# One linear-attention and two-MoE kernel: keys prepared for two pairs of heads together, and split tiles of double size in a ring of two

## The chip, the core and the metric

The kernel runs on one core of one Trainium2 chip. The metric is the device time of one execution in microseconds; three runs of the kernel before took 1551.31, 1551.88 and 1555.19 us, so the median is 1551.88 us. Five engines take part: TensorE (PE; its weight loads are recorded apart, as PEld), VectorE (DVE), ScalarE (ACT), GpSimd (POOL, which here mainly issues DMAs) and SyncE (SP, which issues most DMAs). Each engine runs its own queue in program order, and waits for the others by semaphores.

## The reference, cut to what matters

```python
q_s = exp(q - max(q, axis=-1)); q_s = q_s / (sum(q_s, axis=-1) + 1e-9)   # q, k, v: 8 x 8 x 576 x 64, fp32
k_s = exp(k - max(k, axis=2));  k_s = k_s / (sum(k_s, axis=2) + 1e-9)     # over the 576 positions
kv = einsum('bhsd,bhse->bhde', k_s, v)
x = einsum('bhsd,bhde->bhse', q_s, kv)        # transposed to 4608 tokens x 512
x = relu(x @ w_in)**2 @ w_out                 # 512 -> 2048 -> 512, first layer
x = elu(x @ w_in2) @ w_out2                   # the same sizes, second layer
```

## The kernel before, in words

**Products.** Every fp32 operand of the two layers is split into a high and a low half (fp32r), and a product is three matmuls: high x high, high x low, low x high. The 4608 tokens are nine blocks of 512, t = 0 to 8. In block 0 the first layer is computed directly. From block 1 on, the first product of the layer (`up`, L652 to L654) runs in 16 chunks of 12 matmuls for each block; its result is in one of two banks of PSUM, tag "ph", and ScalarE takes it out with a relu (L661), so TensorE cannot begin chunk c + 2 before the relu of chunk c is done. The second product is a Strassen-Winograd scheme of 7 products on pairs of blocks (1, 2), (3, 4), (5, 6), (7, 8): 56 units u of 6 matmuls (`u_mm`, L773). A unit needs a tile w1 (`u_load`, L751, from the DRAM tensors w1s) and a split of the activations (`u_split`: uh on ScalarE, L760, ul on VectorE, L761). The second layer uses seven products for both matrices (L934, L1049) from 840 us on, and the change doesn't reach into it.

**Attention.** Batch b is 576 positions, its 8 heads are 4 pairs of 128 columns. For each pair: `kt_load` (L244, the transposed keys, one buffer), `k_max` (VectorE, L282, the maximum over the positions, one number per column), `k_load` and `v_load` (L256, L274, two buffers each), `k_row` (one transpose on TensorE, L288, which lays the maxima along a row), `k_sub` (VectorE, L295), `k_exp` (ScalarE, L300), `kv_mm` (L309: ten matmuls of 65 columns that use half of the array's columns each; the extra column of ones in vr gives the sums), `kv_sum`, `kv_inv` (VectorE, three tiny operations) and `kv_out` (ScalarE, two tiny copies with a scale). The rows of maxima, the k-v products, the transposes of q and the x products share two banks of PSUM (tag "att").

**Weight sums.** The Winograd scheme needs seven sums of quarters of the weights, split too. `s_hi` writes a high half with ScalarE (L199, L202), `s_lo` the low half with VectorE (L210, L215), and each half goes to DRAM (w1s, w2s, w3s) by a DMA that GpSimd issues (L203, L216; L211 for the quarter that stands alone, k = 3, where one tile holds both halves). The tiles come from one ring, tag "st", with five buffers of 128 x 512 fp32. The ring also serves the four tiles o of block 0's result (`y_out`, L692 to L695) and the loads of units 2 and 3 (`u_load`; in pair (1, 2) these two take a buffer of another tag, "raw"). A tile of the ring is given out again when the DMA that reads it has landed, or the matmul that reads it is done.

**Order.** Everything is issued in the order in which the code is written; there is no scheduler behind it. `attention(t)` fills 32 slots with the steps of the next key batch and query block. `place_all` and `place_turns` spread the slots over chunks and units of earlier blocks, and the sums of weights, the outputs and the rest of the Winograd additions (`u_out`, `u_rest`) are put at chunks by hand. At each chunk or unit the program emits its matmuls first and then what was put there, so a step that waits on ScalarE holds up the relus behind it, and one on VectorE the splits behind it.

Of the kernel before, what the change touches and what calls it, by code (L numbers as in the profile page):

```python
# [20 lines left out]
def tile_attention_moe_moe2(  # L21
# [172 lines left out]
        return quarters(w, j)[i], s_home(w, j)[:, to]  # L194

    def s_hi(w, j, k):
        hi = pool.tile([P, DM], F32R, tag="st", bufs=5, name=f"sh{w}_{j}_{k}").rearrange("p (i n) -> p i n", n=HW)
        if k == 3:
            nc.scalar.activation(hi[:, 0], s_alone(w, j)[0], AF.Copy)  # L199
        else:  # L200
            x, d = s_source(w, j, k)
            nc.scalar.activation(hi, x, AF.Copy)  # L202
            nc.gpsimd.dma_start(d[:, :, 0, :], f32(hi))  # L203
        parts[w, j, k] = hi

    def s_lo(w, j, k):
        hi = parts.pop((w, j, k))
        if k == 3:
            x, d = s_alone(w, j)
            nc.vector.tensor_tensor(hi[:, 1], x, f32(hi[:, 0]), op=ALU.subtract)  # L210
            nc.gpsimd.dma_start(d, f32(hi))  # L211
        else:
            x, d = s_source(w, j, k)
            lo = pool.tile([P, DM], F32R, tag="st", bufs=5, name=f"sl{w}_{j}_{k}").rearrange("p (i n) -> p i n", n=HW)
            nc.vector.tensor_tensor(lo, x, f32(hi), op=ALU.subtract)  # L215
            nc.gpsimd.dma_start(d[:, :, 1, :], f32(lo))  # L216

    def s_copy(w, j):

# [58 lines left out]
    chunks = ((0, S // P, P), (S // P, SC, S % P))  # L278

    def k_max(b, p):  # L280
        m = att.tile([P, 1], F32, tag="km", bufs=2, name=f"km{b}_{p}")
        nc.vector.tensor_reduce(m, st.pop(("kt", b, p)), axis=AX.X, op=ALU.max)  # L282
        st["km", b, p] = m

# [17 lines left out]
    def kv_mm(b, p):  # L302
        ks, vr = st.pop(("k", b, p)), st.pop(("v", b, p))


        pk = bank([P, D + 1], f"pk{b}_{p}")
        for c in range(SC):
            for j in range(2):
                nc.tensor.matmul(  # L309
                    pk[j * D : (j + 1) * D],  # L310
                    ks[:, c, j * D : (j + 1) * D],
                    vr[:, c, j * (D + 1) : (j + 1) * (D + 1)],
                    start=(c == 0),
                    stop=(c == SC - 1),
                    tile_position=(0, j * D),
                )
        kv = att.tile([P, D], F32, tag="kvs", bufs=2 * NP, name=f"kvs{b}_{p}")
        kvs[b, p] = kv
        st["pk", b, p] = pk

    def kv_sum(b, p):
        z = att.tile([P, 1], F32, tag="kz", bufs=2, name=f"kz{b}_{p}")
# [136 lines left out]
    def attention(t):  # L459

        slots, put = plan()
        new = [b for b, _, _ in pieces(t) if b not in begun]
        begun.update(new)

        far = t > 1
        for b in new:
            for p in range(NP):
                for i, f in (
                    (0, kt_load), (2, k_max), (5, k_load), (5, v_load), (8, k_row), (8, k_sub), (9 + far, k_exp),
                    (11 + far, kv_mm), (11 + far, kv_sum), (11 + far, kv_inv), (11 + 2 * far, kv_out),  # L470
                ):
                    if p == NP - 1 and (f is kv_out if far else i == 11):
                        i = 12
                    if f is kt_load and p and not far:
                        i = (-3, -3, -2)[p - 1]
                    put(i + 4 * p, f, b, p)
        for s in range(NS):
            put(s // 2 if far else (0, 2, 6, 11)[s], q_load, t, s)
            for i, f in (
                (2, q_max), (3, q_sub), (4 + far, q_exp), (5 + 2 * far, q_sum), (6 + 2 * far, q_eps),  # L480
                (7 + 2 * far, q_inv), (7 + 2 * far, q_norm),
            ):
                put(i + 5 * s, f, t, s)
        turns = ((25, 28), (26, None), (29, 31), (30, None)) if far else ((25, 27), (26, None), (28, 29), (28, None))
        for p, (i, j) in enumerate(turns):
            if j is not None:
                put(j, x_mm, t, p)
            put(i, x_tr, t, p)
        return slots
# [8 lines left out]
    )  # L498

    def k0_max(p):  # L500
        m = att.tile([P, 1], F32, tag="km", bufs=2, name=f"km0_{p}")
        nc.vector.tensor_reduce(m, st["kt", 0, p], axis=AX.X, op=ALU.max, negate=True)
        st["km", 0, p] = m

# [171 lines left out]
    def down(layer, t, j):  # L676
# [3 lines left out]
        for c in range(NP):  # L680
# [4 lines left out]
            nc.tensor.matmul(y[c], hi[:, cs], gl, start=False, stop=False)  # L685
            nc.tensor.matmul(y[c], lo[:, cs], gh, start=False, stop=last)
            if last and t < NB - 1:
                y_out(t, c, pool.tile([P, TB], F32, tag="st", bufs=5, name=f"o{layer}_{t}_{c}"))

    def y_out(t, c, o):  # L690
        if c % 2 == 0 or (t, c) == (0, 1):
# [50 lines left out]
    def u_load(t, u):  # L742
        if u < NU:
            i, j = SEVEN[u // NG][0], u % NG
            tag, bufs = ("at", 2) if u < 2 else ("st", 5) if u < 4 else (("xh", "xl")[u % 2] + str(u % 8 // 2), 1)
            if t == PAIRED and 1 < u < 4:
                w = keep.tile([P, 2 * DM], F32R, tag="raw", bufs=3, name=f"w1_{t}_{u}")
                w = w[:, 0:DM].rearrange("p (s k f) -> p s k f", s=2, f=P)
            else:
                w = pool.tile([P, 2, 2, P], F32R, tag=tag, bufs=bufs, name=f"w1_{t}_{u}")  # L750
            nc.sync.dma_start(f32(w), w1s[j][:, i].rearrange("p s (k f) -> p s k f", f=P))  # L751
# [419 lines left out]
    with tc.manual_schedule():  # L1171
# [29 lines left out]
        for t in range(PAIRED, NB - 2, 2):  # L1201
# [14 lines left out]
                place(firsts[t + 2][0], u_out, t, 4, 0, 1, t, m)  # L1216
                place(firsts[t + 2][1], u_out, t, 0, 1, 0, t, m)
            place(firsts[t + 2][2], u_rest, t, 6, 0, t + 1)
            place(firsts[t + 2][4], u_rest, t, "v", 1, t + 1)


        late = [(0, "c", s) for s in (NSL - 2, NSL - 1)] + firsts[1] + firsts[2][:-2]
# [158 lines left out]
```

## Time and profile before

| what | value |
|---|---|
| runs | 1551.31, 1551.88, 1555.19 us, median 1551.88 |
| the profiled execution | 1550.84 us, of which the span of the trace is 1549.1 |
| TensorE busy | 1529.8 us, 99% of the span, granted clock 1.000 |
| VectorE, ScalarE, GpSimd busy | 1226.8 us (79%), 1016.0 us (66%), 129.4 us (8%) |
| chain that ended last | TensorE 87%, VectorE 6%, ScalarE 3%, DMA 2%, issue 1% |
| k-v products, all blocks (L309) | 560 matmuls recorded, 22.5 us busy |
| rows of maxima (L288) | 28 transposes, 8.5 us busy |

How to read it: matmuls are pipelined, so the duration of one in the trace (0.39 us for 512 columns) is longer than the distance between two starts, and the ends are modelled. The cost of something that stands between matmuls is therefore read from starts. A row of the timeline gives the start and the duration in us, the engine, line and operation, "out<-in" by the program's names, the shape, how many instructions are drawn together (x20), and in brackets how long the engine was idle before it and what released it. Two forms of matmul are recorded as two each, so the ten of `kv_mm` stand as x20.

### The profile page before, as it was taken

How to read it: one execution, taken by the hardware profiler on the slowest of the kernel's cores; microseconds unless marked ns; L12 is line 12 of the kernel's file. 1: busy time of each engine (PE TensorE's matmuls, PEld its weight loads, DVE VectorE, ACT ScalarE, POOL GpSimd, SP SyncE). 2: the span in 40 equal slices, each digit the busy share in tenths (PEclk: the TensorE clock that was granted, in tenths of full speed). 3: DMA queues.
4: the chain of work that ended last, by engine and by line, in shares of the span. 5: the costliest groups of instructions: out<-in, count | busy, mean ns of one | idle time of the engine just before them, and what ended most of it. 6: DMA issues, size and time to landing. Idle time of an engine off the chain costs nothing.

```text
span 1549.1 us, 25531 instructions
## 1 busy us (share of the span) xinstructions
PE 1529.8 (99%) x9056; PEld 1320.3 (85%) x9056; DVE 1226.8 (79%) x1803; ACT 1016.0 (66%) x1621; POOL 129.4 (8%) x202
## 2 busy tenths in 40 slices
PE   7999999999999999999999999999999999999999
PEld 5778787877778787887888889988998899999998
DVE  8998597787778787886687897679777976887785
ACT  7976665577565765656564885388538853874873
POOL 1002220032011310032201000000000000000000
PEclk9999999999999999999999999999999999999999
DMA  9857566677576775845686676867676768888876
GB/s 266 252 162 260 204 221 203 236 251 245 168 251 232 260 251 164 263 175 184 219 274 211 196 245 184 242 193 246 185 241 194 234 184 245 276 269 281 262 246 207
DMA packets 200768, 351.68 MB, mean 227 GB/s; under 512 B 20161, under 2 KB 67265, under 8 KB 200641
## 3 DMA queue, kind: packets, MB, share of 16 engines
q1 hardware_dynamic: 186096, 302.71, 64.2%
q0 software_dynamic: 14400, 47.20, 7.7%
q8 instruction: 73, 1.20, 0.3%
q14 instruction: 55, 0.44, 0.1%
q10 hardware_dynamic: 144, 0.13, 0.0%
HBM read 287.05 MB, written 62.91 MB: 226 GB/s over the span
## 4 chain that ended last, share of the span: by engine, by line
PE 87%; DVE 6%; ACT 3%; DMA 2%; issue 1%; POOL 0%; SPq 0%; DVEq 0%; POOLq 0%; ACTq 0%
PE y L1049 23%; PE p L934 22%; PE p L773 17%; PE ph L652 7%; PE ph L653 7%; PE ph L654 7%; PE px L429 1%; PE pk L309 1%; PE pt L401 1%; DVE ul L761 1%; DMA kt<-kt_dram 1%; DVE T L737 0%; DVE B L737 0%; DVE mt_wi L126 0%; ACT raw_wi L120 0%
## 5 line engine op out<-in xcount | busy, mean ns | idle before, releaser
L1049 PE MATMUL y<-w,dh 128*128 128x256 f32 x2016 | 358.7, 281 | 0.0
L934 PE MATMUL p<-x2h,w 128*128 128x512 f32 (+1 forms) x1120 | 322.2, 368 | 0.0
L1049 PEld LDWEIGHTS y<-w,dh 128*128 128x128 f32 x2016 | 309.6, 188 | 0.1
L1049 PE MATMUL y<-w,dl 128*128 128x256 f32 x1008 | 283.9, 282 | 0.2
L773 PE MATMUL p<-uh,w 128*128 128x512 f32 x896 | 281.8, 392 | 0.0
L934 PEld LDWEIGHTS p<-x2h,w 128*128 128x128 f32 x1120 | 207.1, 188 | 27.4 <-DVE g L975 1.1
L652 PE MATMUL ph<-xh,wi0h 128*128 128x512 f32 x576 | 229.6, 399 | 0.0
L653 PE MATMUL ph<-xl,wi0h 128*128 128x512 f32 x576 | 225.1, 391 | 0.7 <-DVE xl L590 0.6
L654 PE MATMUL ph<-xh,wi0l 128*128 128x512 f32 x576 | 224.7, 390 | 0.4 <-DVE wi0l L149 0.3
L934 PE MATMUL p<-x2l,w 128*128 128x512 f32 (+1 forms) x560 | 205.6, 367 | 0.0
L773 PEld LDWEIGHTS p<-uh,w 128*128 128x128 f32 x896 | 168.2, 188 | 36.9 <-issue 2.0
L1049 PEld LDWEIGHTS y<-w,dl 128*128 128x128 f32 x1008 | 189.7, 188 | 1.1 <-DVE dl L1026 0.9
L1020 ACT ACTIVATE dh<-g 128x1024 fp32r<-128x1024 f32 (+1 forms) x120 | 116.3, 974 | 112.0 <-PE y L1049 109.9
L760 ACT ACTIVATE uh<-B 128x512 fp32r<-128x512 f32 x192 | 121.0, 632 | 97.5 <-PE p L773 71.9
L773 PE MATMUL p<-ul,w 128*128 128x512 f32 x448 | 176.2, 393 | 0.7 <-DVE ul L761 0.4
L1026 DVE TENSOR_TENSOR dl<-g,dh 128x1024 fp32r<-128x1024 f32 (+1 forms) x120 | 133.7, 1115 | 45.2 <-ACT dh L1020 44.8
L761 DVE TENSOR_TENSOR ul<-B,uh 128x512 fp32r<-128x512 f32 x192 | 130.3, 688 | 46.2 <-ACT uh L760 45.4
L661 ACT ACTIVATE B<-ph 128x512 f32<-128x512 f32 x128 | 76.3, 596 | 119.9 <-PE ph L654 116.2
L652 PEld LDWEIGHTS ph<-xh,wi0h 128*128 128x128 f32 x576 | 109.0, 189 | 28.4 <-issue 3.9
L654 PEld LDWEIGHTS ph<-xh,wi0l 128*128 128x128 f32 x576 | 108.2, 188 | 24.8 <-DVE wi0l L149 1.6
L653 PEld LDWEIGHTS ph<-xl,wi0h 128*128 128x128 f32 x576 | 108.3, 188 | 22.7 <-DVE xl L590 1.8
L996 DVE SCALAR_TENSOR_TENSOR t<-e,t 128x1024 f32<-128x1024 f32 (+3 forms) x85 | 89.9, 1058 | 33.8 <-ACT e L992 33.4
(155 smaller groups left out, 2298.7 us busy)
## 6 DMA issues: line engine op xcount, KB each, us to landing
w<-w2s SPq DMA_DIRECT2D x280, 256.0 KB, 3.3
w<-w3s SPq DMA_DIRECT2D x280, 256.0 KB, 3.0
w<-w1s SPq DMA_DIRECT2D x224, 256.0 KB, 3.8
raw_wo<-wo_dram SPq DMA_DIRECT2D x32, 512.0 KB, 4.3
vr<-v_dram SPq DMA_DIRECT2D x32, 320.0 KB, 5.8
kt<-kt_dram SPq DMA_DIRECT2D x32, 288.0 KB, 4.2
q<-q_dram SPq DMA_DIRECT2D x36, 256.0 KB, 4.6
ks<-k_dram SPq DMA_DIRECT2D x28, 320.0 KB, 4.7
```

Source lines behind the costliest of these rows:

```text
L652: nc.tensor.matmul(ph, hi[:, c], xh[p], start=(p == 0), stop=False)
L653: nc.tensor.matmul(ph, hi[:, c], xl[p], start=False, stop=False)
L654: nc.tensor.matmul(ph, lo[:, c], xh[p], start=False, stop=(p == NP - 1))
L661: nc.scalar.activation(g, ph, AF.Relu)
L760: nc.scalar.activation(hi, x, AF.Copy)
L761: nc.vector.tensor_tensor(lo, x, f32(hi), op=ALU.subtract)
L773: nc.tensor.matmul(accs[side, m], w[:, s, m], x, start=(new and (j, s) == (0, 0) and x is hi), stop=(j == NG - 1 and s == 1), skip_group_c ...
L934: nc.tensor.matmul(acc, w[:, s, c], x[:, k], start=(begin and (k, s) == (0, 0) and x is hi), stop=((k, s) == (1, 1)), skip_group_check=not ...
L996: nc.vector.scalar_tensor_tensor(g, e, 1.0, g, ALU.add, ALU.mult)
L1020: nc.scalar.activation(hi, x, AF.Copy)
L1026: nc.vector.tensor_tensor(lo, x, f32(hi), op=ALU.subtract)
L1049: nc.tensor.matmul(y2[side, b][:, a * HW : (a + 1) * HW], x[:, u % 2, at], w[:, s], start=(new and (j, s, a) == (0, 0, 0) and x is hi), st ...
```

## The change

1. **Ring.** `s_hi` and `s_lo` share one tile of 128 x 1024 for k = 0, 1, 2, high and low half beside each other for each i; one DMA goes out, after the low half, where there were two. The ring "st" has two buffers of that size, and k = 3 has a buffer of its own, "st1". Two tiles o share one tile of the ring, and so do the loads of units 2 and 3.
2. **Keys of two pairs together, from block t = 2 on (`far`).** `k_rows` makes the rows of maxima of two pairs in one bank, and `kv2_mm` the k-v products of two pairs, with `kv2_sum`, one `kv_inv` and `kv2_out`. km has four buffers. The slots: kt_load 0, 3, 7, 10 (before 0, 4, 8, 12), k_max 3, 6, 10, 13 (before 2, 6, 10, 14), the loads of k and v of both pairs at 7 and 15 (before 5, 9, 13, 17), k_rows 10 and 18, k_sub 10, 11, 18, 19, k_exp 12, 13, 20, 21, the product at 15 and 23, its copies at 16 and 24.
3. **Block 1** (not `far`): of the last pair, k_load, v_load, k_row, k_sub, k_exp and kv_out come one slot earlier, kv_mm, kv_sum and kv_inv two.
4. **`u_rest`**: the sum v and its two DMAs stand at chunk 9 of the block after the pair, where they stood at chunk 4.

**The diff** (lines that are only "..." stand for what is left out; kv2_sum adds 1e-9 to the two sums as kv_sum does).

```diff
--- before.py
+++ after.py
...
         return quarters(w, j)[i], s_home(w, j)[:, to]
 
     def s_hi(w, j, k):
-        hi = pool.tile([P, DM], F32R, tag="st", bufs=5, name=f"sh{w}_{j}_{k}").rearrange("p (i n) -> p i n", n=HW)
         if k == 3:
+            hi = pool.tile([P, DM], F32R, tag="st1", name=f"sh{w}_{j}_{k}").rearrange("p (i n) -> p i n", n=HW)
             nc.scalar.activation(hi[:, 0], s_alone(w, j)[0], AF.Copy)
         else:
-            x, d = s_source(w, j, k)
-            nc.scalar.activation(hi, x, AF.Copy)
-            nc.gpsimd.dma_start(d[:, :, 0, :], f32(hi))
+            hi = pool.tile([P, 2 * DM], F32R, tag="st", bufs=2, name=f"sh{w}_{j}_{k}")
+            hi = hi.rearrange("p (i s n) -> p i s n", s=2, n=HW)
+            nc.scalar.activation(hi[:, :, 0], s_source(w, j, k)[0], AF.Copy)
         parts[w, j, k] = hi
 
     def s_lo(w, j, k):
...
             nc.gpsimd.dma_start(d, f32(hi))
         else:
             x, d = s_source(w, j, k)
-            lo = pool.tile([P, DM], F32R, tag="st", bufs=5, name=f"sl{w}_{j}_{k}").rearrange("p (i n) -> p i n", n=HW)
-            nc.vector.tensor_tensor(lo, x, f32(hi), op=ALU.subtract)
-            nc.gpsimd.dma_start(d[:, :, 1, :], f32(lo))
+            nc.vector.tensor_tensor(hi[:, :, 1], x, f32(hi[:, :, 0]), op=ALU.subtract)
+            nc.gpsimd.dma_start(d, f32(hi))
 
     def s_copy(w, j):
 
...
-        m = att.tile([P, 1], F32, tag="km", bufs=2, name=f"km{b}_{p}")
+        m = att.tile([P, 1], F32, tag="km", bufs=NP, name=f"km{b}_{p}")
...
+
+    def k_rows(b, p):
+        pm = bank([P, 2 * P], f"pm{b}_{p}")
+        for i in range(2):
+            row = st["pm", b, p + i] = pm[:, i * P : (i + 1) * P]
+            nc.tensor.transpose(row, st.pop(("km", b, p + i)).to_broadcast([P, P]), ident)
+
+    def kv2_mm(b, p):
+        pk = bank([P, 2 * (D + 1)], f"pk{b}_{p}").rearrange("p (i n) -> p i n", i=2)
+        for i in range(2):
+            ks, vr = st.pop(("k", b, p + i)), st.pop(("v", b, p + i))
+            for c in range(SC):
+                for j in range(2):
+                    nc.tensor.matmul(
+                        pk[j * D : (j + 1) * D, i],
+                        ks[:, c, j * D : (j + 1) * D],
+                        vr[:, c, j * (D + 1) : (j + 1) * (D + 1)],
+                        start=(c == 0),
+                        stop=(c == SC - 1),
+                        tile_position=(0, j * D),
+                    )
+        st["pk", b, p] = pk
+
...
+    def kv2_out(b, p):
+        pk, z = st.pop(("pk", b, p)), st.pop(("kz", b, p))
+        for i in range(2):
+            kv = kvs[b, p + i] = att.tile([P, D], F32, tag="kvs", bufs=2 * NP, name=f"kvs{b}_{p + i}")
+            for j in range(2):
+                r = slice(j * D, (j + 1) * D)
+                nc.scalar.activation(kv[r], pk[r, i, 1 - j : 1 - j + D], AF.Copy, scale=z[r, i : i + 1])
 
     def kv_sum(b, p):
         z = att.tile([P, 1], F32, tag="kz", bufs=2, name=f"kz{b}_{p}")
...
         far = t > 1
         for b in new:
             for p in range(NP):
+                if far:
+                    put((0, 3, 7, 10)[p], kt_load, b, p)
+                    put((3, 6, 10, 13)[p], k_max, b, p)
+                    h = p // 2 * 8
+                    if p % 2 == 0:
+                        put(10 + h, k_rows, b, p)
+                    for f, i in ((k_load, 7), (v_load, 7), (k_sub, 10 + p % 2), (k_exp, 12 + p % 2)):
+                        put(i + h, f, b, p)
+                    if p % 2:
+                        for i, f in ((15, kv2_mm), (15, kv2_sum), (15, kv_inv), (16, kv2_out)):
+                            put(i + h, f, b, p - 1)
+                    continue
                 for i, f in (
-                    (0, kt_load), (2, k_max), (5, k_load), (5, v_load), (8, k_row), (8, k_sub), (9 + far, k_exp),
-                    (11 + far, kv_mm), (11 + far, kv_sum), (11 + far, kv_inv), (11 + 2 * far, kv_out),
+                    (0, kt_load), (2, k_max), (5, k_load), (5, v_load), (8, k_row), (8, k_sub), (9, k_exp),
+                    (11, kv_mm), (11, kv_sum), (11, kv_inv), (11, kv_out),
                 ):
-                    if p == NP - 1 and (f is kv_out if far else i == 11):
-                        i = 12
-                    if f is kt_load and p and not far:
+                    if p == NP - 1:
+                        i -= f in (k_load, v_load, k_row, k_sub, k_exp, kv_mm, kv_sum, kv_inv)
+                    if f is kt_load and p:
                         i = (-3, -3, -2)[p - 1]
                     put(i + 4 * p, f, b, p)
         for s in range(NS):
...
     )
 
...
             if last and t < NB - 1:
-                y_out(t, c, pool.tile([P, TB], F32, tag="st", bufs=5, name=f"o{layer}_{t}_{c}"))
+                if c % 2 == 0:
+                    st["o"] = pool.tile([P, 2, TB], F32, tag="st", bufs=2, name=f"o{layer}_{t}_{c}")
+                y_out(t, c, st["o"][:, c % 2])
 
     def y_out(t, c, o):
         if c % 2 == 0 or (t, c) == (0, 1):
...
     def u_load(t, u):
         if u < NU:
             i, j = SEVEN[u // NG][0], u % NG
-            tag, bufs = ("at", 2) if u < 2 else ("st", 5) if u < 4 else (("xh", "xl")[u % 2] + str(u % 8 // 2), 1)
-            if t == PAIRED and 1 < u < 4:
-                w = keep.tile([P, 2 * DM], F32R, tag="raw", bufs=3, name=f"w1_{t}_{u}")
-                w = w[:, 0:DM].rearrange("p (s k f) -> p s k f", s=2, f=P)
+            tag, bufs = ("at", 2) if u < 2 else (("xh", "xl")[u % 2] + str(u % 8 // 2), 1)
+            if u == 2:
+                two, tag, bufs = (keep, "raw", 3) if t == PAIRED else (pool, "st", 2)
+                ops["two"] = two.tile([P, 2 * DM], F32R, tag=tag, bufs=bufs, name=f"w1_{t}_{u}")
+            if 1 < u < 4:
+                w = ops["two"][:, (u - 2) * DM : (u - 1) * DM].rearrange("p (s k f) -> p s k f", s=2, f=P)
             else:
                 w = pool.tile([P, 2, 2, P], F32R, tag=tag, bufs=bufs, name=f"w1_{t}_{u}")
             nc.sync.dma_start(f32(w), w1s[j][:, i].rearrange("p s (k f) -> p s k f", f=P))
...
                 place(firsts[t + 2][0], u_out, t, 4, 0, 1, t, m)
                 place(firsts[t + 2][1], u_out, t, 0, 1, 0, t, m)
             place(firsts[t + 2][2], u_rest, t, 6, 0, t + 1)
-            place(firsts[t + 2][4], u_rest, t, "v", 1, t + 1)
+            place(firsts[t + 2][9], u_rest, t, "v", 1, t + 1)
 
 
         late = [(0, "c", s) for s in (NSL - 2, NSL - 1)] + firsts[1] + firsts[2][:-2]
```

**The order, place 1: TensorE in block 1's chunks 4 to 7** (`ph0_1_4` is chunk 4 of block 1, `pm2_1` the row of maxima of batch 2's pair 1, `pk2_1` the k-v product of that pair). Before, a product ends chunk 4 and a row stands right behind it:

```order
L653 MATMUL ph0_1_4_1622<-xl0_1_3_1421,wi0h4_523 128x512
L654 MATMUL ph0_1_4_1622<-xh0_1_3_1420,wi0l4_524 128x512
L309 MATMUL pk2_0_1638<-vr0_122,ks2_0_1546 64x65 x10
L288 MATMUL pm2_1_1654<-ident_115,km2_1_1550 128x128
L652 MATMUL ph0_1_5_1671<-xh0_1_0_1399,wi0h5_592 128x512
L653 MATMUL ph0_1_5_1671<-xl0_1_0_1400,wi0h5_592 128x512
```

and two chunks later the same again, for pair 1. After, two rows stand alone behind chunk 3, and the products of both pairs alone behind chunk 6:

```order
L701 MATMUL ph0_1_3_1586<-xh0_1_3_1420,wi0l3_479 128x512
L324 MATMUL pm2_0_1603<-ident_115,km2_0_1495 128x128
L324 MATMUL pm2_0_1603<-ident_115,km2_1_1543 128x128
L699 MATMUL ph0_1_4_1617<-xh0_1_0_1399,wi0h4_523 128x512
L700 MATMUL ph0_1_4_1617<-xl0_1_0_1400,wi0h4_523 128x512
```

```order
L701 MATMUL ph0_1_6_1673<-xh0_1_3_1420,wi0l6_657 128x512
L332 MATMUL pk2_0_1689<-vr0_122,ks2_0_1565 64x65 x10
L332 MATMUL pk2_0_1689<-vr1_125,ks2_1_1568 64x65 x10
L699 MATMUL ph0_1_7_1734<-xh0_1_0_1399,wi0h7_721 128x512
L700 MATMUL ph0_1_7_1734<-xl0_1_0_1400,wi0h7_721 128x512
```

The row has left the product's place, and two products (`pk2_0` holds both pairs') have moved into one. In the whole order, from batch 2 on, there were 18 products with a row behind them, 6 products alone and 6 rows alone; now 12 double products and 12 double rows stand apart.

**Place 2: ScalarE at the end of block 0** (`o0_0_0` is a tile of block 0's result, `shwo0_4_2` the third high half of weight column 4's sums, `B11` the relus of `up`). Before, three o tiles, a step of q and the high half, then the relus of chunks 2 and 3:

```order
L692 ACTIVATE o0_0_0_1525<-y0_0_0_533 128x512
L692 ACTIVATE o0_0_1_1531<-y0_0_1_537 128x512
L692 ACTIVATE o0_0_2_1537<-y0_0_2_541 128x512
L358 ACTIVATE q2_0_1430<-q2_0_1430 128x512
L202 ACTIVATE shwo0_4_2_1552<-sumswo0_4_1461 128x512
L661 ACTIVATE B11_1_1_1571<-ph0_1_2_1558 128x512
L663 ACTIVATE B11_1_1_1571<-B11_1_1_1571 128x512
```

After:

```order
L741 ACTIVATE o0_0_0_1523<-y0_0_0_533 128x512
L741 ACTIVATE o0_0_0_1523<-y0_0_1_537 128x512
L741 ACTIVATE o0_0_2_1534<-y0_0_2_541 128x512
L393 ACTIVATE q2_0_1430<-q2_0_1430 128x512
L203 ACTIVATE shwo0_4_2_1545<-sumswo0_4_1461 128x2x256
L708 ACTIVATE B11_1_1_1562<-ph0_1_2_1549 128x512
L710 ACTIVATE B11_1_1_1562<-B11_1_1_1562 128x512
```

The order is the same, but two o tiles are now halves of one buffer, and the turn of the ring is `shwo0_4_1`, `o0_0_0`, `o0_0_2`, `shwo0_4_2`, so that `shwo0_4_2` takes the buffer of `o0_0_0`.

**Place 3: SP in the units of pair (1, 2)** (`w1_1_36` is the load of unit 36, `kt4_1` the transposed keys of batch 4's pair 1, `raw_wi1_0` a column of weights). Before:

```order
L751 DMA w1_1_35_3024<-w1s3_101 128x512
L751 DMA w1_1_36_3040<-w1s4_102 128x512
L109 DMA raw_wi1_0_3047<-wi1_dram 128x1024
L751 DMA w1_1_37_3055<-w1s5_103 128x512
L244 DMA kt4_1_3061<-kt_dram 128x576
L751 DMA w1_1_38_3069<-w1s6_104 128x512
L751 DMA w1_1_39_3081<-w1s7_105 128x512
```

After:

```order
L802 DMA w1_1_35_2965<-w1s3_101 128x512
L243 DMA kt4_1_2975<-kt_dram 128x576
L802 DMA w1_1_36_2983<-w1s4_102 128x512
L109 DMA raw_wi1_0_2990<-wi1_dram 128x1024
L802 DMA w1_1_37_2998<-w1s5_103 128x512
L802 DMA w1_1_38_3010<-w1s6_104 128x512
L802 DMA w1_1_39_3022<-w1s7_105 128x512
```

`kt4_1` has moved ahead of `w1_1_36`, `raw_wi1_0` and `w1_1_37`.

## Rows read from the trace of the kernel before

**Rows 1.** The page: busy time of the engines, and the chain that ended last

```profile
PE 1529.8 (99%) x9056; PEld 1320.3 (85%) x9056; DVE 1226.8 (79%) x1803; ACT 1016.0 (66%) x1621; POOL 129.4 (8%) x202
...
PE 87%; DVE 6%; ACT 3%; DMA 2%; issue 1%; POOL 0%; SPq 0%; DVEq 0%; POOLq 0%; ACTq 0%
```

**Rows 2.** Timeline of TensorE (start us, us, engine, line): product and row

```profile
322.21 0.39 PE L654 MATMUL ph<-xh,wi0l 128*128 128x512 f32 x1
...
322.89 0.39 PE L654 MATMUL ph<-xh,wi0l 128*128 128x512 f32 x1
323.21 0.80 PE L309 MATMUL pk<-vr,ks 128*64 128x65 f32 x20
323.95 0.32 PE L288 MATMUL pm<-ident,km 128*128 128x128 f32 x1
...
324.35 0.39 PE L653 MATMUL ph<-xl,wi0h 128*128 128x512 f32 x1
```

**Rows 3.** Timeline of TensorE, a product alone

```profile
341.41 0.39 PE L654 MATMUL ph<-xh,wi0l 128*128 128x512 f32 x1
341.73 0.80 PE L309 MATMUL pk<-vr,ks 128*64 128x65 f32 x20
...
342.79 0.39 PE L653 MATMUL ph<-xl,wi0h 128*128 128x512 f32 x1
```

**Rows 4.** Timeline of TensorE, a row of maxima alone

```profile
192.21 0.39 PE L654 MATMUL ph<-xh,wi0l 128*128 128x512 f32 x1
192.44 0.27 PE L288 MATMUL pm<-ident,km 128*128 128x128 f32 x1
...
192.78 0.40 PE L653 MATMUL ph<-xl,wi0h 128*128 128x512 f32 x1
```

**Rows 5.** Timeline of TensorE, eight transposes of q

```profile
163.44 0.39 PE L654 MATMUL ph<-xh,wi0l 128*128 128x512 f32 x1
163.66 1.04 PE L401 MATMUL pt<-ident,q 128*128 128x128 f32 x8
...
164.77 0.39 PE L653 MATMUL ph<-xl,wi0h 128*128 128x512 f32 x1
```

**Rows 6.** Timeline of the weight loads (PEld) before the product alone

```profile
341.19 0.19 PEld L654 LDWEIGHTS ph<-xh,wi0l 128*128 128x128 f32 x1
341.73 0.66 PEld L309 LDWEIGHTS pk<-vr,ks 128*64 128x64 f32 x20 [0.35 <-issue]
```

**Rows 7.** Timeline near 280 us, VectorE and then TensorE

```profile
279.83 0.75 DVE L282 TENSOR_REDUCE km<-kt 128x1 f32<-128x576 f32 x1 [1.87 <-DMA kt<-kt_dram]
...
280.26 0.61 PE L773 MATMUL p<-uh,w 128*128 128x512 f32 x2
281.24 0.50 PE L773 MATMUL p<-ul,w 128*128 128x512 f32 x1 [0.36 <-DVE ul L761]
```

**Rows 8.** Timeline near 132 us, ScalarE, GpSimd; landing of L695's DMAs

```profile
132.82 0.64 ACT L202 ACTIVATE shwo<-sumswo 128x512 fp32r<-128x512 f32 x1
...
131.75 2.33 POOL L695 DMA_DIRECT2D x2d<-o  x4 [3.52 <-ACT o L692]
...
DMA to landing us min/median/max: 2.3/2.7/4.1
```

**Rows 9.** Timeline of ScalarE near 331 and 511 us, of TensorE at 333

```profile
330.88 0.63 ACT L202 ACTIVATE shwi<-sumswi 128x512 fp32r<-128x512 f32 x1 [1.38 <-DMA w2s<-shwi]
...
332.68 0.60 ACT L661 ACTIVATE B<-ph 128x512 f32<-128x512 f32 x1
...
333.34 0.50 PE L652 MATMUL ph<-xh,wi0h 128*128 128x512 f32 x1
...
511.01 0.61 ACT L202 ACTIVATE shwi<-mt_wi 128x512 fp32r<-128x512 f32 x1
...
514.97 0.42 ACT L199 ACTIVATE shwi<-mt_wi 128x256 fp32r<-128x256 f32 x1 [1.85 <-DMA w2s<-slwi]
```

**Rows 10.** Timeline of VectorE near 142 us

```profile
142.44 0.88 DVE L295 TENSOR_TENSOR ks<-ks,pm 128x512 f32<-128x512 f32 x2 [0.46 <-DMA ks<-k_dram]
```

More of the change, by code (lines that the diff above doesn't have):

```diff
@@ L319, in kv_mm, with kv2_sum @@
         st["pk", b, p] = pk
+    def k_rows(b, p):
[18 more added lines that the diff above has]
+        st["pk", b, p] = pk
+    def kv2_sum(b, p):
+        z = st["kz", b, p] = att.tile([P, 2], F32, tag="kz2", bufs=2, name=f"kz{b}_{p}")
+        pk = st["pk", b, p]
+        nc.vector.tensor_scalar(z[0:D], pk[0:D, :, 0], 1e-9, None, ALU.add)
+        nc.vector.tensor_scalar(z[D:P], pk[D:P, :, D], 1e-9, None, ALU.add)
+    def kv2_out(b, p):
[5 more added lines that the diff above has]
+                nc.scalar.activation(kv[r], pk[r, i, 1 - j : 1 - j + D], AF.Copy, scale=z[r, i : i + 1])
     def kv_sum(b, p):
@@ L500, in k0_max @@
     def k0_max(p):
-        m = att.tile([P, 1], F32, tag="km", bufs=2, name=f"km0_{p}")
+        m = att.tile([P, 1], F32, tag="km", bufs=NP, name=f"km0_{p}")
         nc.vector.tensor_reduce(m, st["kt", 0, p], axis=AX.X, op=ALU.max, negate=True)
```

## The prediction, as it was put on record

> **What bounds the kernel now.** I read the page first: the share of the span that TensorE is busy, and the chain that ended last. TensorE works 1529.8 of 1549.1 us and the chain is 87% TensorE [rows 1], so only two things can move the time: work that leaves TensorE's queue, and gaps in it that open or close. A change on ScalarE, VectorE, GpSimd or the queues counts only where TensorE ends up waiting. Next I read the timeline of TensorE around each kind of interruption of the main stream, and the starts in it, since the ends are modelled: a main matmul starts every 0.227 us ((322.89 - 322.21) / 3 [rows 2]). Then I took the waits of TensorE and followed those that come from VectorE, ScalarE or a DMA back to the tile that was late.
>
> **Part 1: fewer interruptions of TensorE.** An interruption is costed from the start of the last main matmul before it to the start of the second main matmul after it (the first one after it is late as well), less the two steps of 0.227 that would have passed anyway.
> - A k-v product (10 matmuls, 20 rows of the trace) with a row of maxima right behind it: 324.35 - 322.89 = 1.46, less 0.45, is 1.00 us [rows 2].
> - A k-v product alone: 342.79 - 341.41 - 0.45 = 0.93 us [rows 3].
> - A row of maxima alone: 192.78 - 192.21 - 0.45 = 0.12 us [rows 4].
> - Eight transposes in one go: 164.77 - 163.44 - 0.45 = 0.88, so 0.11 us each [rows 5].
>
> From block 2 on there are 24 pairs of heads. By TensorE's order before, their 48 steps make 18 products with a row behind them, 6 products alone and 6 rows alone: 18 x 1.00 + 6 x 0.93 + 6 x 0.12 = 24.3 us. After there are 12 double products and 12 double rows, none beside the other. A double row is two transposes, 0.22 us. A double product has no row. It cannot cost less than a single one plus the time in which 20 more recorded matmuls pass: a run of 20 is 0.80 us from first start to last end, with 0.20 to 0.22 of that the tail of the last one, so 0.6 [rows 2, 3]; 0.93 + 0.60 = 1.53 us. It cannot cost more than two single ones, 1.86. I take 1.53, since nothing in the rows interrupts a run once it is under way, while the entry shows a gap: the first weight load of the product starts 0.35 us after the one before has ended, where the loads of main matmuls follow each other at 0.23 [rows 6]. So 12 x (1.53 + 0.22) = 21.0 us, **-3.3 us**; at the upper bound 12 x (1.86 + 0.22) = 25.0, +0.7 us.
>
> By that row the entry fee is real, and paying it 12 times instead of 24 times is the whole gain. The Trainium skill, "TensorE: Matmul & The Clock Gate", section "Step-by-step: what each phase is for", says that the engine pulls weight loads ahead of matmuls in flight when their row groups don't conflict or the spare weight buffer is free. By that rule there would be no fee to save (rival D); the row of 0.35 us speaks against it here.
>
> **Part 2: keys loaded earlier.** In block 3's units VectorE stood 1.87 us before the maximum of kt, for the DMA that loads it, and the ul split behind it in VectorE's queue came late; TensorE lost 281.24 - 280.26 - 0.46 = 0.52 us [rows 7]. SP's order now has that load three DMAs earlier (ahead of w1_36, raw_wi1_0 and w1_37). Those three DMAs have to be worth the 1.87 us that VectorE stood; SP issues about one load of w1 per unit of 1.4 us (six matmuls), so they are: **-0.5 us**, and 0 at the least if SP itself is held by the buffers of w1. What is late next there is the wait that stands on every unit, ul behind uh, which is short enough that TensorE shows none.
>
> **Part 3: the ring of split tiles.** Five tiles of 512 columns become two of 1024. Each holds the high and the low half, and goes out in one DMA, after the low half. The DMAs that fall away (64) are issued by GpSimd, which is 8% busy: nothing on the path. The cost is the ring. A new high half (ScalarE) must wait until the DMA of the tile two places back has landed, and behind it in ScalarE's queue stand the relus that free TensorE's two ph banks. I set the start of each item in the trace of before against the landing of what will be its predecessor in the ring of two. Ten places come out negative, nine on ScalarE and one (a load of w1) on SP, with 12.6 us in all on ScalarE. The first is at the end of block 0: the four o tiles are written out from 131.75 on, the second of them at about 132.3, and a landing takes 2.7, so 135.0, while shwo at 132.82 wants that tile: 2.1 us [rows 8]. The largest is at 511.01, where a high half would now wait for the very transfer that in before released ScalarE at 514.97: 3.9 us [rows 9]. The other seven lie between 0.2 and 2.3.
>
> What does TensorE pay? In before ScalarE already waited 1.38 us for such a DMA at 330.88; the relu behind it began at 332.68, ended at 333.28, and TensorE began the chunk that needs that bank at 333.34 [rows 9]. So about 1.4 us is what the two banks cover there, and from there TensorE pays. The four waits over 1.4 (3.9, 2.3, 2.1, 1.8) have an excess of 4.4 us together; a neighbour in a stretch where VectorE is full (block 1's second quarter, where it already waits for ks [rows 10]) may add 1. Bounds 0 to 5.4 us. I take **+1.5**: of the two such waits that the trace holds, the one of 1.38 cost TensorE about 0.1 us and the one of 1.85 [rows 9] nothing, since it fell early in a chunk, which pulls the estimate to the lower half; but the largest of the new ones is twice as long as either.
>
> **Part 4: the rest.** Block 1's last pair comes one or two slots earlier, the v sum of y moves five chunks on: VectorE's 1.2 us and two DMAs, with nobody waiting for x2d in the same pair. 36 small VectorE operations fall away on an engine at 79%. All at nothing; covered by TensorE's stream, and if that cover is gone no more than one VectorE operation of 0.9 us [rows 10], once per block.
>
> **Sum.** -3.3 - 0.5 + 1.5 = -2.3 us. The profiled execution took 1550.84 us, 1.04 under the median of the runs, 1551.88. Against the profile that is 1548.5, against the median 1549.6. I predict 1549.6.
>
> **The rivals.**
> - **B, no new waits.** ScalarE's waits vanish in the slack of the banks, -3.8 us: 1548.1. For it: the waits of 1.38 and 1.85 cost almost nothing. Against it: three waits are longer. If other small stalls at the starts of units go too (together no more than about 1 us), 1547.
> - **C, the ring is the new bound.** Each us that ScalarE waits is paid by TensorE: 1551.9 - 3.8 + 12.6 = 1560.7, slower. It decides when more than two thirds of the 12.6 are paid (8.5 us). For it: in block 1, and in weight sums near 335 and 511 us, a relu stands right behind the waiting copy, and a transfer of double size may land later than the low half's did. Against it: the two banks cover some 1.4 us of each.
> - **D, merging saves nothing.** The double product costs two single ones: 1551.9 + 0.7 - 0.5 + 1.5 = 1553.6. Against it: the gap of 0.35 at the entry.
> - **E, loads in a bunch.** The k and v loads of two pairs (1.28 MB) now come together, right behind the double product that frees their buffers. If the second ks lands late, k_sub waits at the head of VectorE's queue, ul or xl come late and TensorE stands. In before the wait for ks was 0.46 [rows 10]; 1.5 us in each of the six key blocks would be 9 us: 1559, slower.
>
> **How the numbers follow.** About 0.3% (4.7 us) is what a measurement of this kernel can tell from no change; faster is under 1547.2, slower over 1556.5. Forecast 0.48, B 0.20 within the bound and 0.12 under it, D 0.08, C 0.08, E 0.04. So faster 0.12, same 0.76, slower 0.12. The range goes from B with the smaller stalls gone and the runs' spread of about 1 us, 1546.0, to the forecast with all 5.4 us of the ring paid and D's price for the merging, 1551.9 + 0.7 - 0.5 + 5.4 = 1557.5, cut to 1556.0 since both ends together are unlikely.
>
> **What would show it.** Right: around a double product the starts of main matmuls lie 1.98 us apart (1.53 + 0.45) and around a double row 0.67; VectorE's wait for kt near 280 us is gone; ScalarE shows waits for a DMA of about 2 us near 133 and 335 and near 4 us at 511, with TensorE's stalls near them 1.5 us in all. Wrong: a double product of 2.3 us from start to start (D), waits of VectorE for ks of over 1 us in several blocks (E), or TensorE stalls over 5 us behind relus (C).

## The result, and the profile after

The changed kernel takes 1562.41 us (median of four runs, 1560.66 to 1563.85) against 1551.88: 1.0068 times the time before, 95% interval 1.0055 to 1.0082. That is 10.5 us slower, where 2.3 us less was forecast, and outside the range (1546.0 to 1556.0). The profiled execution has a span of 1559.7 us.

The page of the changed kernel, busy time and the chain that ended last, against [rows 1]:

```profile
PE 1531.7 (98%) x9056; PEld 1325.1 (85%) x9056; DVE 1221.4 (78%) x1767; ACT 1013.7 (65%) x1621; POOL 76.5 (5%) x138
...
PE 80%; DVE 8%; issue 6%; DMA 2%; ACT 2%; POOL 1%; SPq 0%; DVEq 0%; POOLq 0%; ACTq 0%
```

VectorE, ScalarE and GpSimd work less, and TensorE's busy time grows by 1.9 of the 10.6 us by which the span does: it waits more. The merged steps cost what was worked out. Timeline of TensorE around a double product and a double row, against [rows 2 to 4]:

```profile
145.78 0.39 PE L701 MATMUL ph<-xh,wi0l 128*128 128x512 f32 x1
146.10 1.39 PE L332 MATMUL pk<-vr,ks 128*64 128x65 f32 x40
...
147.76 0.39 PE L700 MATMUL ph<-xl,wi0h 128*128 128x512 f32 x1
...
150.05 0.39 PE L701 MATMUL ph<-xh,wi0l 128*128 128x512 f32 x1
150.28 0.38 PE L324 MATMUL pm<-ident,km 128*128 128x128 f32 x2
...
150.73 0.39 PE L700 MATMUL ph<-xl,wi0h 128*128 128x512 f32 x1
```

147.76 - 145.78 = 1.98 us and 150.73 - 150.05 = 0.68, where 1.98 and 0.67 were forecast. Costed in this way from starts, all products and rows of maxima from block 2 on took 24.4 us before and take 21.1 after: -3.3 us, as forecast. The maximum of kt no longer waits either (VectorE, against [rows 7]):

```profile
282.11 0.75 DVE L281 TENSOR_REDUCE km<-kt 128x1 f32<-128x576 f32 x1
```

The same row in two later runs that have this load in its old slot, the ring alone and then the last experiment (whose code is that of the kernel before up to block 7):

```profile
282.21 0.75 DVE L281 TENSOR_REDUCE km<-kt 128x1 f32<-128x576 f32 x1 [0.90 <-DMA kt<-kt_dram]
```

```profile
280.27 0.75 DVE L282 TENSOR_REDUCE km<-kt 128x1 f32<-128x576 f32 x1 [0.22 <-DMA kt<-kt_dram]
```

There the wait is 0.90 and 0.22 us in place of 1.87, and TensorE shows no stop behind it.

To see where the time went, I set the start of each main matmul of the trace after against the same one (by its number in the stream, 7968 in both) of the trace before. The difference jumps at five places, given with the time after and the jump: **156 us (+4.4), 231 (+1.8), 335 (+5.3), 480 (+1.0), 521 (+5.3)**, 17.8 us together. At 156, 335 and 521 the jump takes in a double product right behind the stop, whose cost comes back later in the stream. One more jump lies in block 0: +4.9 us up to 94 us, where a k-v product of block 1's last pair waits 2.28 us for its exp and the clock falls; by 130 us the difference is back at 0.0. Elsewhere it falls on the whole, and ends at +10.7. A stop is given below as the distance between two starts less 0.227; the bracket of the row shows a little less, since it counts from the modelled end. TensorE at four of the five places, and the first rows after the stop at 156:

```profile
155.75 0.39 PE L701 MATMUL ph<-xh,wi0l 128*128 128x512 f32 x1
158.05 0.50 PE L699 MATMUL ph<-xh,wi0h 128*128 128x512 f32 x1 [1.92 <-ACT B L708]
...
159.14 0.63 PE L700 MATMUL ph<-xl,wi0h 128*128 128x512 f32 x1
159.57 0.63 PE L701 MATMUL ph<-xh,wi0l 128*128 128x512 f32 x1
160.00 0.63 PE L699 MATMUL ph<-xh,wi0h 128*128 128x512 f32 x1
...
233.48 0.47 PE L824 MATMUL p<-uh,w 128*128 128x512 f32 x1 [1.74 <-DMA w<-w1s]
...
338.73 0.50 PE L699 MATMUL ph<-xh,wi0h 128*128 128x512 f32 x1 [2.86 <-ACT B L708]
...
524.52 0.79 PE L699 MATMUL ph<-xh,wi0h 128*128 128x512 f32 x1 [2.99 <-ACT B L708]
```

A stop of 2 to 3 us is not all: behind three of them matmuls start 0.43 us apart (159.57 - 159.14) in place of 0.227. The view by windows of those stretches shows the granted clock there (the columns are the window, its length, busy time of TensorE, weight loads, VectorE, ScalarE, GpSimd, then the granted clock, the share of the DMA engines and GB/s):

```profile
158.10:161.80 3.70, 3.70 (x11) 2.91 (x12) 1.29 (x2) 3.67 (x8) 0.25 (x1) 0.62 1.09 387
338.70:343.00 4.30, 4.27 (x12) 3.39 (x13) 4.23 (x10) 2.87 (x6) 0.28 (x1) 0.64 0.58 203
524.50:527.40 2.90, 2.88 (x7) 2.31 (x8) 2.87 (x9) 2.90 (x6) 0.57 (x1) 0.50 0.44 179
```

Half of the full clock (0.50) is the lower level, 1.2 GHz of 2.4; the first two windows take in some of the full clock as well. Some 20 matmuls ran at the lower level, 0.2 us lost on each. So: five stops of 2.08 + 1.90 + 3.03 + 0.87 + 3.15 = 11.0 us, 4.0 for the slow clock, less 3.3 for the merged steps and 0.5 at kt: +11.2, against the +10.7 that was measured. Block 0 adds nothing by 130 us. (In its first 60 us the traces differ by some us from one execution to the next.)

Who held the relus? ScalarE at those three places:

```profile
157.40 0.60 ACT L708 ACTIVATE B<-ph 128x512 f32<-128x512 f32 x1 [5.17 <-DMA w1s<-wo]
...
336.46 0.63 ACT L203 ACTIVATE shwi<-sumswi 128x512 fp32r<-128x512 f32 x1 [5.03 <-DMA w2s<-shwi]
...
523.35 0.63 ACT L203 ACTIVATE shwi<-mt_wi 128x512 fp32r<-128x512 f32 x1 [5.64 <-DMA w2s<-shwi]
```

The last two are high halves that wait for the ring, with the relus behind them, at the places of [rows 9], but for 5.0 and 5.6 us, where about 2 and 3.9 were worked out. (The one near 133 is 1.3 us, where 2.1 were.) The first is no ring: the relu itself writes into a tile (a former w_out column) that a DMA of `s_copy` still reads. SP's timeline there, after and then before:

```profile
146.98 0.35 SPq L255 DMA_DIRECT2D ks<-k_dram  x1
147.38 0.55 SPq L273 DMA_DIRECT2D vr<-v_dram  x1
148.03 1.26 SPq L255 DMA_DIRECT2D ks<-k_dram  x1
149.34 0.55 SPq L273 DMA_DIRECT2D vr<-v_dram  x1
149.95 7.89 SPq L220 DMA_DIRECT2D w1s<-wo  x9
```

```profile
141.48 0.33 SPq L256 DMA_DIRECT2D ks<-k_dram  x1
141.86 0.55 SPq L274 DMA_DIRECT2D vr<-v_dram  x1
142.46 2.35 SPq L221 DMA_DIRECT2D w1s<-wo  x3
```

SP now stands for the double product, which frees both buffers of ks (the view of SP's waits gives 4.1 us), and the copies go out at 149.95, behind four loads, instead of 142.46.

### The profile page after: what moved, and what is told of

It is laid out like the page before. It is cut to its first block, busy times and chain, and to the rows that moved or that the text cites. A ratio compares the mean times of both kernels' runs of the same rounds, so it can differ in the third digit from the quotient of the medians.

```text
span 1559.7 us, 25314 instructions
## 1 busy us (share of the span) xinstructions
PE 1531.7 (98%) x9056; PEld 1325.1 (85%) x9056; DVE 1221.4 (78%) x1767; ACT 1013.7 (65%) x1621; POOL 76.5 (5%) x138
## 4 chain that ended last, share of the span: by engine, by line
PE 80%; DVE 8%; issue 6%; DMA 2%; ACT 2%; POOL 1%; SPq 0%; DVEq 0%; POOLq 0%; ACTq 0%
PE y L1100 23%; PE p L985 22%; PE p L824 16%; PE ph L699 5%; PE ph L701 5%; PE ph L700 5%; DVE ul L812 1%; DMA w2s<-shwi 1%; PE px L464 1%; PE pt L436 1%; PE pk L332 1%; POOL w1s L215 1%; DVE mt_wi L126 1%; DVE qm L384 0%; DVE T L786 0%
```

## The experiments

The first theory (A) after this reading: the ring of two makes the stops at 231, 335 and 521, and SP's order the one at 156. The rival (R): the loads of two pairs in a bunch make every DMA in their stretch late, and the ring only passes it on. The first two expectations use the letters so; from the fifth on, "theory A" stands for the bunch, that is for R. Results are ratios to the kernel before, from runs on the same chip.

**Each half of the change alone.** The first has only the hunks on keys (`k_max`, `k_rows`, `kv2_*`, `attention`), the second only those on `s_hi`, `s_lo`, `y_out` and `u_load`.

> The kernel before with the new keys alone (rows and k-v products of two pairs together, new slots, block 1's last pair earlier); the ring of five split tiles, two DMAs per tile and the v sum at chunk 4 as before. In the trace of the changed kernel four places make it slower, by starts of the same main matmuls: +4.4 us at 156 us (a relu behind w1s<-wo), +1.8 at 231 (loads of w1), +5.2 at 335 and +5.2 at 521 (ScalarE behind a DMA of the ring). Theory A: the last three come from the ring of two, so they vanish here and the first one stays: 1562.4 - 12.2 = 1550.2, between 1548 and 1552. Rival R: the k and v loads of two pairs in a bunch delay everything behind them whatever the ring is, so the stalls stay: 1558 or more.

Measured: 1556.19 us, 1.0024 (1.0013 to 1.0035). Neither expectation holds in full. The stop at 521 is gone, but 156 stays (2.6 us, and the slow clock), so does 231 (1.93), and at 335 there are still 1.67 us, behind a high half that waited 3.66 us with a ring of five.

> The kernel before with the new ring alone (two tiles of 128x1024, one DMA for both halves, o tiles and loads of units 2 and 3 in pairs); keys and v sum as before. Theory A, the ring alone is enough: TensorE stalls of 2 to 4 us near 335 and 511 us with a slow clock behind each, 1556 to 1562. Rival R, the ring only hurts where the bunched loads make its DMAs land 3 to 4 us later: at most one stall over 1 us, 1551 to 1554.

Measured: 1553.11 us, 1.0005 (0.9996 to 1.0015), and no stop of TensorE over 0.5 us after block 0. ScalarE near 133, 335 and 511 us, and the longest stop of TensorE behind it:

```profile
138.29 0.63 ACT L203 ACTIVATE shwo<-sumswo 128x512 fp32r<-128x512 f32 x1 [2.04 <-DMA x2d<-o]
...
334.01 0.63 ACT L203 ACTIVATE shwi<-sumswi 128x512 fp32r<-128x512 f32 x1 [1.80 <-DMA w2s<-shwi]
...
516.84 0.63 ACT L203 ACTIVATE shwi<-mt_wi 128x512 fp32r<-128x512 f32 x1 [2.08 <-DMA w2s<-shwi]
...
336.46 0.51 PE L651 MATMUL ph<-xh,wi0h 128*128 128x512 f32 x1 [0.27 <-ACT B L660]
```

So with the loads as before, the waits for the ring that the prediction listed do come, at 2.0, 1.8 and 2.1 us (2.1, about 2 and 3.9 were forecast), and cost TensorE 0.4 us at the most. 0.24% plus 0.05% make less than the 0.68% of both, and less than the 0.54% of both with the v sum where these two have it (the next run): each half makes the other dearer. R is ahead.

**The v sum back at chunk 4**

```diff
-            place(firsts[t + 2][9], u_rest, t, "v", 1, t + 1)
+            place(firsts[t + 2][4], u_rest, t, "v", 1, t + 1)
```

> The changed kernel with the v sum of y and its two DMAs back at chunk 4. In the changed kernel other transfers of y (4 of 256 KB) stand right ahead of the ring's DMA near 327 and 513 us, two of them from this kind of step. If their place in GpSimd's queue makes the ring's landing late: the stalls at 335 and 521 shrink by half, 1562.4 - 5 = 1557. If it is the k and v loads or the ring's depth alone: 1562, within 1.5 us.

Measured: 1560.62 us, 1.0054 (1.0037 to 1.0071). The stops at 335 and 521 are 2.78 and 2.37 us instead of 3.03 and 3.15. The v sum has a small part in them, no more, and the time lies within 1.5 us of 1562, the second case. The stop at 156 is missing in this profile, though nothing is edited ahead of block 3: of the four profiles with that order of SP's queue (after, the keys alone with and without block 1's edit, this one) three have it. Here the relu waits 2.47 us for the copy in place of 5.17, and TensorE doesn't stop; why it waits less was not followed.

**The copies ahead of the key loads**

```diff
-                place(late[at + d], f, "wo0", *a)
+                if f is s_copy:
+                    extras.setdefault(late[at], []).insert(0, (f, ("wo0", *a)))
+                else:
+                    place(late[at + d], f, "wo0", *a)
```

> The changed kernel with the DMAs that copy w_out's quarters to w1s (s_copy) written ahead of the chunk's key loads, so that on SP they no longer stand behind loads of k and v that wait 4.1 us for the double product. Theory: the stall at 156 us (relu behind w1s<-wo, 2.1 us, and the slow clock behind it) goes, -4.4: 1558.0. Rival: the relu only waits for another buffer or transfer next, and the time stays at 1562 within 1.5 us.

Measured: 1561.58 us, 1.0057 (1.0042 to 1.0072): the rival. The stop at 156 is gone and another has come at 141. ScalarE and TensorE there:

```profile
142.57 0.63 ACT L203 ACTIVATE shwo<-sumswo 128x512 fp32r<-128x512 f32 x1 [4.50 <-DMA x2d<-o]
...
143.74 0.50 PE L699 MATMUL ph<-xh,wi0h 128*128 128x512 f32 x1 [2.12 <-ACT B L708]
```

The four key loads now meet the o tiles' DMAs, which land 6.5 us after their issue instead of the 2.7 of [rows 8], and the ring of two hands this to ScalarE. It is the wait that the prediction placed here, at twice its price.

**The same order with the ring of five**

> The new keys alone with the old ring of five, and the copies of w_out's quarters to w1s written ahead of the chunk's key loads. With the new ring this order moved the loads of k and v earlier, and the o tiles' DMAs behind them landed 6.5 us after their issue, so that ScalarE stood 4.5 us for the ring. Theory A (bunched loads make DMAs late, a shallow ring turns that into waits): with five tiles that wait doesn't exist, and the stall at 156 us behind w1s<-wo goes as well: 1556.2 - 4.8 = 1551.4. Rival: the stall at 156 only moves, 1556 within 1.5 us.

Measured: 1554.06 us, 1.0018 (1.0005 to 1.0030). No stop at 141 or 156; one of 2.26 us at 332 with slow matmuls behind it, and 1.96 at 228 and 1.54 at 476. The expected 4.8 us do not show in the times: the ratio falls by 0.06%, less than its interval, since other stops came as that one went.

**Half of the bunch left out**

```diff
-        nc.sync.dma_start(vr[:, :, 1 : P + 1], v[b, p])
+        if b < 2:
+            nc.sync.dma_start(vr[:, :, 1 : P + 1], v[b, p])
```

> The changed kernel without the loads of v from block 2 on (old values are used; half of the 1.28 MB that comes in a bunch is left out). Theory A: landings near 156, 327 and 514 us shorten by some 2 us, and the stalls of 2 to 3 us there, which draw a slow clock behind them, mostly go: 1562.4 - 8 = 1554. Rival, the depth of the ring or SP's wait for the double product alone: the stalls stay, 1560 or more.

Measured: 1550.36 us, 0.9990 (0.9980 to 1.0000), with the ring of two still in place: 12 us less than the changed kernel, more than the 8 expected. The stops at 156 and 521 are gone, 0.6 us is left at 331, and 1.87 at 227. That speaks for the bunch (R) and against the ring's depth alone. The kernel before without v was not run, so a part of the 12 us may be the smaller traffic as such; the next experiment moves all bytes. The view of DMAs (queue, count, KB each, median us from issue to landing) between 322 and 334 us before, in the same window after, and between 317 and 329 us here, where the same transfers come some 4 us earlier:

```profile
w2s<-shwi POOLq DMA_DIRECT2D x4, 256.0 KB, 4.5
```

```profile
w2s<-shwi POOLq DMA_DIRECT2D x2, 512.0 KB, 8.0
...
ks<-k_dram SPq DMA_DIRECT2D x2, 320.0 KB, 3.5
vr<-v_dram SPq DMA_DIRECT2D x2, 320.0 KB, 6.1
```

```profile
w2s<-shwi POOLq DMA_DIRECT2D x2, 512.0 KB, 4.9
```

The two ring DMAs of double size take 4.9 us (median) to land when the v loads are away and 8.0 when they are there; the half-size ones took 4.5 before. Their size is not what made them late.

**v three slots later**, all else as in the changed kernel:

```diff
-                    for f, i in ((k_load, 7), (v_load, 7), (k_sub, 10 + p % 2), (k_exp, 12 + p % 2)):
+                    for f, i in ((k_load, 7), (v_load, 10), (k_sub, 10 + p % 2), (k_exp, 12 + p % 2)):
```

> The changed kernel with the loads of v three slots later (10 and 18 in place of 7 and 15), so that the 1.28 MB of two pairs comes as two times 0.64 MB. Theory A (the bunch makes the DMAs of the ring and of the copies late): as without v at all, the stalls at 156, 335 and 521 us mostly go, 1552 to 1556. Rival: v then only comes late itself, the double product waits for it, and the time stays over 1559.

Measured: 1554.41 us, 1.0020 (1.0009 to 1.0031). By the ratios, one number gives back 0.48 of the 0.68%, some 7.5 us, with all bytes still moved. The stops at 156 and 521 are gone; at 335 one of 3.5 us stays, since v now meets the ring there (the two v loads of that stretch land in 10.1 us).

**What stays: block 1's last pair, and the stop at 231.** The first takes the new keys with the old ring and puts block 1's last pair back (`if p == NP - 1 and i == 11: i = 12`); the second writes every weight step ahead of the keys' steps of its chunk.

> The new keys alone with the old ring, and block 1's last pair back in its old slots. In every trace with the earlier slots TensorE loses about 3 us more near 90 us (the product waits for exp of ks) and gets back 2 to 3 us up to 142 us. If they cancel: 1556 within 1 us of the same without this edit. If the earlier slots cost: 1553 to 1555.

Measured: 1554.83 us, 1.0017 (1.0006 to 1.0029); the same without the edit had 1.0024 (1.0013 to 1.0035). The intervals overlap, so the first case, they cancel, is not refuted. By starts, the ten traces with the earlier slots lose 0.7 to 1.2 us against the trace of before between 85 and 130 us; this one gains 0.4 there, but the ring alone, without those slots, loses 1.1. A cost of about 1 us is likely, not shown.

> The new keys alone with the old ring, and in every chunk the weight sums' steps written ahead of the keys' and queries' steps. In the keys-only trace the last column's sums come 3.6 us later than before on VectorE, behind two subtractions of keys and four steps of q, and units 0 to 7 of pair (1, 2) wait for it: 1.85 us at 234. If VectorE's order is the cause there and near 335: these go, and the copy to w1s no longer stands behind k and v: 1556.2 - 1.9 - 1.5 - 4.8 = 1548. If the loads are the cause whatever the order: 1554 or more.

Measured: 1558.54 us, 1.0040 (1.0028 to 1.0052): a miss. The stop at 231 even grows to 2.15 us; the one near 335 goes, others come at 138 (2.18), 515 (0.65) and 710 (1.76). Order within a chunk alone is not the cause at 231. By the count of main matmuls, the last subtraction (VectorE) of these sums begins 7 matmuls later with the keys alone than before, and the DMA behind it lands 9 later, which is 2.0 us.

**The last sums earlier**, on top of the ring of five, the copies first and v later:

```diff
-        at = 0
-        for j in FREED:
+        for at, j in zip((0, 4, 8, 12, 16, 20, 23, 26), FREED):
```

> The new keys alone with the old ring, the copies to w1s ahead of the key loads, and v three slots later. Without the last of these the trace lost 1.9 us at 228, 4.4 near 332 and 1.6 at 476. Theory A: the one at 332 and the one at 476 go, 1554.1 - 5 = 1549, at or a little under the kernel before (1551.6). Rival: 1553 or more.

Measured: 1552.07 us, 1.0007 (0.9994 to 1.0021), between the two cases. No stop at 476; 1.62 us left at 332, 1.80 at 228.

> As e10_keys_copy_v_later, and the sums of w_out's last two columns one and two chunks earlier. The wait of 1.9 us at 228 us (units of pair (1, 2) behind loads of w1, behind the last column's sums) stays in every kernel with the new keys. If the sums' place is its cause it goes: 1549 - 1.9 = 1547, faster than before by 0.3%. If not: as e10_keys_copy_v_later.

Measured: 1550.62 us, 0.9992 (0.9983 to 1.0002). The stop at 228 is gone, so the place of the last sums was its cause. The 1547 of the expectation is missed: the kernel is no slower than the one before, and not shown to be faster; 2.0 us are left near 335. From the keys alone (1.0024) to this run the intervals part; the single steps between them show in the traces, not in the times.

**The slow clock by itself**

```diff
+    GRADED = {(7, 4): 6, (7, 9): 7, (7, 14): 8, (8, 2): 9, (8, 6): 10, (8, 10): 11}
...
-        nc.scalar.activation(g, ph, AF.Relu)
+        for _ in range(GRADED.get((t, j), 1)):
+            nc.scalar.activation(g, ph, AF.Relu)
```

> The kernel before with the relu of six single chunks of blocks 7 and 8 repeated 6, 7, 8, 9, 10 and 11 times (same values), so that TensorE stands for a bank of ph between about 0.6 and 3.4 us, in steps of 0.55. In the other traces stalls of 1.7 to 1.9 us were followed by matmuls 0.227 us apart and stalls of 2.1 us or more mostly by seven or eight matmuls 0.427 us apart (granted clock 0.83 over 10 us in place of 1.00). If the length of the stall decides: the short ones here cost their own time only, the long ones 1.5 us more each. If something else in those places decides (a DMA, the engines' load): no slow matmuls here at all.

Measured: 1582.68 us, 1.0202 (1.0179 to 1.0224). The six stops were 2.9, 1.9, 3.4, 3.2, 3.8 and 4.4 us, longer than planned, so only one of them is short. Two of them, and the windows behind them and behind the third:

```profile
691.95 0.50 PE L654 MATMUL ph<-xh,wi0h 128*128 128x512 f32 x1 [2.70 <-ACT B L664]
...
709.19 0.50 PE L654 MATMUL ph<-xh,wi0h 128*128 128x512 f32 x1 [1.75 <-ACT B L664]
```

```profile
692.00:695.50 3.50, 3.50 (x9) 2.78 (x10) 1.42 (x3) 3.00 (x6) 1.02 (x3) 0.55 0.69 265
709.20:712.70 3.50, 3.50 (x18) 2.93 (x19) 2.63 (x7) 3.45 (x7) 0.61 (x2) 1.00 0.18 75
730.80:736.00 5.20, 5.20 (x12) 3.79 (x13) 3.31 (x6) 1.88 (x4) 0.00 (x0) 0.50 0.00 0
```

The stop of 1.9 us kept the full clock, the five longer ones lost it, also where no DMA moved (share 0.00). So TensorE's own stop is enough.

## Why the prediction was wrong, point by point

- **Interruptions (part 1): right.** The double product takes 1.98 us from start to start, to the hundredth, and the double row 0.68; over all of them the gain is 3.3 us. Rival D is out; the price of entry is real and is paid half as often.
- **Keys earlier (part 2): the number came, the reason is not shown.** The wait for kt is gone, and the difference falls by 0.5 us there, as forecast. But in two other executions with the load in its old slot VectorE waits 0.90 and 0.22 us and TensorE doesn't stop. The 0.5 us was read from one execution, and is not shown to be the change's doing.
- **The ring (part 3): right place, wrong size, and this is the step that failed.** It set starts of the trace of before against landings *of the trace of before*. The change itself moved the loads, and the landings of the ring's DMAs near 327 us went from 4.5 to 8.0 us. The wait at 511 was forecast at 3.9 us and came as 5.6, the one near 335 at about 2 and came as 5.0. The term was +1.5 us; behind these two waits TensorE lost 6.2 us in stops and 2.6 to the slow clock. The ring alone, with the loads as before, cost 0.05% (not distinguishable from nothing), in line with the +1.5 us.
- **The bunch of loads: seen as rival E, with the wrong victim.** E had the bytes (1.28 MB) and the moment right, but priced only VectorE's wait for ks. Those who paid were the other transfers of the stretch. C and E were written as two cases with a chance each; they are one case, since E makes the landings for which C makes ScalarE wait. That C's 1560.7 lies near the measured time is luck: it had every us of 12.6 paid by TensorE, where 6.2 of the 10.7 us that ScalarE waited for w2s came through, and the rest of the loss comes from places that C didn't have.
- **SP's queue: a step that was left out.** Part 2 followed kt on SP, but no part asked what stands behind the k load of batch 2's pair 2, which waits for the double product. It is `s_copy`, and a relu needs its tile: a stop of 2.1 us at 156 in this trace, and 1.4 for the slow clock. Moving the copies alone brought the key loads forward and the stop with them (to 141), so the order of SP's queue and the bunch are one cause there, and no run parts them.
- **The place of the last sums** (231 us, 1.9 us): not seen. Their last subtraction comes 7 main matmuls later once the keys' steps stand in other chunks; putting the sums one and two chunks earlier removed the stop.
- **The slow clock: not in the sum.** Every us of a stop was priced at one us. The three stops with slow matmuls behind them cost 1.2 to 1.4 us more each.
- **The rest (part 4), at nothing:** block 1's earlier slots cost perhaps 1 us, and the v sum's new place at most a small part; neither is clear of the intervals. The stop at 480 us (0.9 us) is gone without the v loads and with later ones; what makes it was not followed.

The sum with the sizes measured: -3.8 of parts 1 and 2, +11.0 of stops, +4.0 of slow clock, together +11.2, against +10.7 between the two traces.

In the version that is level with the kernel before, a high half still waits 4.0 us near 335 us, and the view names VectorE for it; one step earlier (the sums in their old place) it is 3.6 us, for a DMA of the ring. What holds it there is left open.

## What to carry to other kernels

Merging two small steps saves an entry on the bound engine, but with two buffers it also makes their loads come at one moment; count what else must land in that stretch, and what stands behind the waiting load on its queue. When a change moves transfers, landings from the trace of before are no price for a shallower ring. And price a stop of the bound engine by its length first: here those under 1.97 us cost themselves, longer ones often half as much again.

## What the runs showed of the hardware

- A transfer's landing depended on what else moved more than on its size: near 327 us, 256 KB landed in 4.5 us before, 512 KB in 4.9 without and in 8.0 with 0.64 MB of loads of v.
- TensorE's granted clock fell from full to half (2.4 to 1.2 GHz) behind its own stops. Over all the traces, leaving block 0 out, of the stops up to 1.96 us none was followed by a run of slow matmuls, of those between 1.97 and 2.8 us 8 of 13 were, and every one of 2.86 us or more was; a run was 6 to 12 matmuls of 0.43 us. This agrees with the Trainium skill, "TensorE: Matmul & The Clock Gate", section "What's actually happening", in that the clock has two levels and falls after idling. The price, 0.2 us for each of these matmuls and so 1.2 to 2.4 us for a run, comes from the rows here.
